# Attention with a top-32 mask and a highway FFN: the pair maxima read PSUM, one evacuation per pair, preparation in pieces late in each period, FFN steps inside the list chain

## The chip, the cores and the metric

The kernel runs on one core of a Trainium2 chip. The metric is device time in microseconds (us) for one launch. The core's engines are TensorE (PE), VectorE (DVE), ScalarE (ACT), GpSimd (POOL) and SyncE (SP), which here only issues DMAs.

## The reference

Attention over 8 batches, 8 heads, 576 rows and a head width of 64, in which each row keeps its 32 largest scores, and then a highway FFN with d_model = 512 on the 4608 rows:

```python
scores = scale * np.matmul(q, k.transpose(0, 1, 3, 2))
kth = np.partition(scores, -top_k, axis=-1)[..., -top_k:-top_k + 1]   # top_k = 32
scores = np.where(scores >= kth, scores, -1000000000.0)
scores = scores - np.max(scores, axis=-1, keepdims=True)
attn = np.exp(scores)
attn = attn / (np.sum(attn, axis=-1, keepdims=True) + 1e-09)
x = np.matmul(attn, v)                  # heads side by side: 4608 x 512
H = np.maximum(x @ w_h, 0.0)
T = 1.0 / (1.0 + np.exp(-(x @ w_t + b_t)))
out = T * H + (1.0 - T) * x
```

## The kernel before

A tile is 128 query rows of one head against all 576 keys. Two tiles make a pair, and there are 144 pairs: 18 for each of the 8 batches. The rows of a batch are cut into groups: four groups of 128 rows with four pairs each, and one remaining group of 64 rows, in whose tiles two heads lie side by side, with two pairs. The main loop runs one step for each pair n, and in this text a step is called a period. Every compute engine takes its instructions in exactly the order in which the loop writes them, so the order of the calls in the loop is the schedule.

What happens to pair n is spread over several periods. `scores` makes q times k for two tiles into two PSUM tiles `ps` (TensorE), and `evac` takes them through a ReLU into the SBUF tile `z` (ScalarE, one instruction for each tile); both are written one period ahead. In period n, `tree` takes the maximum of the two halves of `z` as `hi` and of the two halves of `hi` as `hh` (VectorE), and `minima` makes the matching minima `hl` and `lo` by integer subtraction and addition (GpSimd, four instructions). In period n+1, `lists` runs a chain of MAX8 and MATCH_REPLACE8 for both tiles in turn, which finds the 32nd largest score (`m`, `w`; VectorE). In period n+2, `mask` makes the penalty `pen` = ReLU(threshold - z) (ScalarE), and `trans` transposes z and subtracts a steep multiple of `pen` in PSUM (`zr`, `zt`; TensorE, twenty products), and ScalarE takes the exponential as `et`. In period n+3, `av` multiplies `et` with v and a column of a constant that gives the row's sum (TensorE), and ScalarE copies the result to `xs`.

When a group's last pair has passed `av`, `norm` takes the reciprocal `rinv` (VectorE) and makes `x` (GpSimd), and three FFN jobs are queued, of which each period takes one, behind `lists`: `ffn_x` transposes x (`xtps`), `ffn_h` multiplies with w_h (`hps`) and makes `d` (VectorE), and `ffn_t` multiplies with w_t (`tps`), takes the tanh (ScalarE), updates `d` (VectorE) and adds up `o` (GpSimd, two additions: `o<-x` and `o<-o,d`), which a DMA on SyncE writes. The transposes of x, the three products and those of the preparation share one PSUM tile, `fp`, which has one buffer. `settle` (GpSimd: `room`, `slack`, `reach`) gathers a check for each group; should it fail, an exact version of the whole kernel runs behind the main loop.

The preparation of the next batch, `prep_pair`, loads k, q and v of two heads (`kin`, `qin`, `vin`; twelve DMAs on SyncE), transposes k and q on TensorE (`kqps`) and copies them and v with ScalarE. It is called as a whole, in four of the 18 periods, ahead of that period's `scores`:

```python
            if n in preparing:
                prep(*preparing[n])
            if n == 1:
                load_weights()
            ...
            if have(n + 1):
                g, pi = pairs[n + 1]
                ops.scores(n + 1, g, pi, preps[g.b])
                ops.evac(n + 1)
            if have(n - 1):
                ops.lists(n - 1, *pairs[n - 1])
            for job in ffn[:1]:
                job.pop(0)()
```

The functions that the diff touches, with the lines of the profile (the recording layer at line 35 stands for nearly all instructions there, so rows are told apart by their tiles):

Of the kernel before, what the change touches and what calls it, by code (L numbers as in the profile page):

```python
# [19 lines left out]
J = 4  # L20
# [42 lines left out]
class Ops:  # L63


    def __init__(self, ctx, tc, shared, exact):
# [18 lines left out]
        self.bigps = pool("bigps", 2, space=PS)  # L85
# [7 lines left out]
    def load_pair(self, src, hp, name):  # L93
        nc, D, S, R, P = self.nc, self.D, self.S, self.R, self.P
        JP = J * P
        t = self.ldpool.tile([P, J + 1, 2, D], FP32, tag=name, name=name)
        for hh in range(2):
            h = 2 * hp + hh
            nc.sync.dma_start(
                t[:, 0:J, hh, :], src(h, 0, JP).rearrange("(p j) d -> p j d", j=J)  # L100
            )
            nc.sync.dma_start(t[0:R, J, hh, :], src(h, JP, S))
        return t
# [6 lines left out]
    def prep_pair(self, srcs, hp, prep):  # L110
# [3 lines left out]
        kin = self.load_pair(srcs[1], hp, "kin")  # L114
        qin = self.load_pair(srcs[0], hp, "qin")
        vin = self.load_pair(srcs[2], hp, "vin")
        for src_t, dst_t in ((kin, kT), (qin, qT)):
            kqps = self.fps.tile([P, 512], FP32, tag="fp", name="kqps")
            for c in range(J):
                nc.tensor.transpose(  # L120
                    kqps[:, c * P : (c + 1) * P],
                    src_t[:, c, :, :].rearrange("p h d -> p (h d)"),
                    self.ident[:],
                )
            nc.scalar.copy(dst_t[:, hp, 0:JP], kqps[:])
        kqps = self.fps.tile([P, 512], FP32, tag="fp", name="kqps")
        for i, src_t in enumerate((kin, qin)):
            nc.tensor.transpose(
                kqps[:, i * R : (i + 1) * R],
                src_t[0:R, J, :, :].rearrange("p h d -> p (h d)"),  # L130
                self.ident[0:R, 0:R],
            )
        for i, dst_t in enumerate((kT, qT)):
            nc.scalar.copy(dst_t[:, hp, JP:S], kqps[:, i * R : (i + 1) * R])
        vdst = vb[:, 2 * hp : 2 * hp + 2, :, 0:D].rearrange("p h c d -> p c h d")
        nc.scalar.copy(vdst[:, 0:J], vin[:, 0:J])
        nc.scalar.copy(vdst[0:R, J], vin[0:R, J])
# [3 lines left out]
    def scores(self, n, g, pi, prep):  # L141
# [3 lines left out]
        pss = [  # L145
            self.bigps.tile([P, (J + 1) * P], FP32, tag="big", name="ps")
            for _ in range(2)
        ]
        for s0, s1 in ((0, 512), (512, S)):
            for ti, heads in enumerate(g.pairs[pi]):  # L150
                for hi, h in enumerate(heads):
# [3 lines left out]
                        pss[ti][rows, s0:s1],  # L155
# [3 lines left out]
        self.st[n] = dict(pss=pss)  # L159

    def evac(self, n):
        nc, P, S = self.nc, self.P, self.S
        pss = self.st[n].pop("pss")
        if self.exact:
            sc = self.scpool.tile([P, 2, S], FP32, tag="sc", name="sc")
        else:
            sc = self.zbufs[n % NZ][:, :, 0:S]
        for ti in range(2):
            if self.exact:
                nc.scalar.copy(sc[:, ti, :], pss[ti][:, 0:S])  # L170
            else:
                nc.scalar.activation(sc[:, ti, :], pss[ti][:, 0:S], AF.Relu)
        self.st[n]["sc"] = sc

    def tree(self, n):
# [7 lines left out]
        nc.vector.tensor_tensor(hi[:], sc[:, :, 0:H1], sc[:, :, H1:S], ALU.max)  # L183
# [67 lines left out]
    def lists(self, n, g, pi):  # L251
# [16 lines left out]
        while gens:  # L268
            gens = [x for x in gens if next(x, 0) is None]
# [128 lines left out]
    def ffn_x(self, g):  # L398
# [11 lines left out]
        )  # L410

    def ffn_h(self, g):

        nc, P, n_g, ql = self.nc, self.P, self.n_g, g.qlen
        hps = self.fps.tile([P, 512], FP32, tag="fp", name="hps")
        for i in range(n_g):
            nc.tensor.matmul(
                hps[0:ql, :],
# [15 lines left out]
    def ffn_t(self, g):  # L434

        nc, P, n_g, ql = self.nc, self.P, self.n_g, g.qlen
        tps = self.fps.tile([P, 512], FP32, tag="fp", name="tps")
        for i in range(n_g):
            nc.tensor.matmul(
                tps[0:ql, :],  # L440
# [6 lines left out]
            tps[0:ql, :], self.cst[:, 0:ql], self.bt[:], start=False, stop=True  # L447
        )
        nc.scalar.activation(tps[0:ql, :], tps[0:ql, :], AF.Tanh)
        nc.vector.scalar_tensor_tensor(  # L450
            out=g.d[0:ql, :],
            in0=tps[0:ql, :],
# [6 lines left out]
    def ffn_o(self, g, dst):  # L459
        gp, ql = self.nc.gpsimd, g.qlen  # L460
        o = self.fpool.tile([self.P, self.dm], FP32, tag="o", name="o")
        gp.tensor_tensor(o[0:ql, :], g.x[0:ql, :], g.x[0:ql, :], ALU.add)
        gp.tensor_tensor(o[0:ql, :], o[0:ql, :], g.d[0:ql, :], ALU.add)
# [4 lines left out]
def kernel(  # L468
# [43 lines left out]
    for i in range(2):  # L512
        vt = const([P, H, nck, DE], BF16, f"v{i}")
        nc.gpsimd.memset(vt[:], 2.0)
# [20 lines left out]
    with ExitStack() as cm:  # L535
# [4 lines left out]
        def load_weights():  # L540
            for src, dst in ((moe_w_h, wh), (moe_w_t, wt)):
                for i in range(0, n_g, 2):
# [5 lines left out]
                    weights.append((w32, dst[:, i : i + 2, :], 1.0))  # L548
# [5 lines left out]
            weights.append((bt32, bt[:].unsqueeze(1), 0.5))  # L554
# [24 lines left out]
        preps = {}  # L579

        def prep(b, hp):
            if hp == 0:
                preps[b] = ops.prep_alloc(vbufs[b % 2])
            ops.prep_pair(srcs(b), hp, preps[b])

        preparing = {hp - 1: (0, hp) for hp in range(1, NHP)}
        for b in range(1, B):
            for hp in range(NHP):
                preparing[first[b] - 12 + 3 * hp] = (b, hp)
# [5 lines left out]
        prep(0, 0)  # L595
        ops.scores(0, *pairs[0], preps[0])
        ops.evac(0)
        ffn = []
        step = 0
        while step < NPR + 4 or ffn:  # L600
            n = step
            if have(n):
                ops.tree(n)
                ops.minima(n)
            if have(n - 2):
                ops.mask(n - 2, *pairs[n - 2], tis=(0,))
            if have(n - 3):
# [4 lines left out]
            if n in preparing:  # L612
                prep(*preparing[n])
            if n == 1:
# [112 lines left out]
```

## Time and profile before

| | |
|---|---|
| median of 3 runs | 1103.97 us (1099.82 to 1106.38) |
| the profiled execution | 1100.31 us, of which the trace spans 1098.5 us |
| busy: VectorE, GpSimd, TensorE, ScalarE | 976.7, 839.6, 822.1, 712.1 us |
| mean granted TensorE clock | 0.859 of full speed |
| instructions | 20764 |

Busy time is the union of an engine's instructions. The profile names for each idle time of an engine what ended it, and TensorE's clock is given as a share of full speed.

### The profile page before, as it was taken

To read this page: it belongs to the slowest core of one execution; us is meant where nothing else is said; L and a number is where in the kernel's file an instruction comes from. 1 tells how busy PE (TensorE), PEld (TensorE's weight loads), DVE (VectorE), ACT (ScalarE), POOL (GpSimd) and SP (SyncE) were. 2 spreads that over 40 slices of the span, in tenths; PEclk is the share of its full clock that TensorE was granted. 3 is DMA by queue.
4 is the path that set the end of the run, shared out by engine and by line. 5 is a ranking of instruction groups with operands and counts; after the bars stand their busy time and mean duration, and the time that the engine had idled before them with its cause. 6 is when DMAs were issued, how large, how long until landed. Compare 5 with 4: busy or idle time off the path is not lost.

```text
span 1098.5 us, 20764 instructions
## 1 busy us (share of the span) xinstructions
PE 822.1 (75%) x6562; PEld 549.7 (50%) x6601; DVE 976.7 (89%) x4162; ACT 712.1 (65%) x1425; POOL 839.6 (76%) x842
## 2 busy tenths in 40 slices
PE   5667788778877787777877768786787778777764
PEld 3445455455545555455554545554455445555542
DVE  2699999989998999889998899988999888999992
ACT  3567676667766676567666666676676666766652
POOL 6598788867886778777787777877778776888872
PEclk9988898878887889788897888978799787989886
DMA  4611200122002210121101111011110110000000
GB/s 109 171 34 43 61 25 10 44 59 55 11 17 53 53 44 11 32 57 45 34 10 48 43 43 43 11 38 43 48 39 11 38 43 10 11 11 7 10 20 18
DMA packets 123333, 41.54 MB, mean 38 GB/s; under 512 B 117456, under 2 KB 117456, under 8 KB 123216
## 3 DMA queue, kind: packets, MB, share of 16 engines
q1 hardware_dynamic: 123216, 40.14, 14.6%
q8 instruction: 54, 0.88, 0.3%
q14 instruction: 63, 0.52, 0.2%
HBM read 30.67 MB, written 9.44 MB: 37 GB/s over the span
## 4 chain that ended last, share of the span: by engine, by line
DVE 70%; PE 17%; ACT 8%; issue 3%; SPq 1%; DMA 1%; POOL 0%; ACTq 0%; DVEq 0%; POOLq 0%
DVE w L35 30%; DVE m L35 18%; DVE hh L35 9%; DVE hi L35 8%; PE ps L35 7%; PE kqps L35 5%; DVE d L35 4%; PE tps L35 2%; ACT pen L35 2%; ACT qT L35 2%; ACT kT L35 1%; PE hps L35 1%; ACT tps L35 1%; ACT z L35 1%; PE zt L35 1%
## 5 line engine op out<-in xcount | busy, mean ns | idle before, releaser
L35 ACT ACTIVATE pen<-z,m 128x576 bf16<-128x576 f32 x288 | 223.2, 775 | 142.7 <-DVE m L35 142.7
L35 PE MATMUL ps<-kT,qT 64*128 64x64 f32 (+3 forms) x1280 | 244.6, 509 | 0.0
L35 PE MATMUL zt<-ident,z 128*128 128x128 f32 x1152 | 238.1, 300 | 0.0
L35 DVE MAX8 m<-w 128x8 f32<-128x168 f32 (+1 forms) x864 | 232.6, 309 | 0.0
L35 POOL TENSOR_TENSOR hl<-hi,hh 128x288 int32<-128x288 int32 x144 | 114.2, 793 | 152.7 <-DVE hh L35 152.7
L35 PE MATMUL zt<-nident,pen 128*128 128x128 bf16 x1152 | 226.4, 233 | 0.0
L35 ACT ACTIVATE z<-ps 128x576 f32<-128x576 f32 x288 | 170.9, 646 | 65.1 <-PE ps L35 61.6
L35 POOL TENSOR_TENSOR lo<-lo,z 128x576 int32<-128x576 int32 x144 | 203.6, 1414 | 11.3
L35 POOL TENSOR_TENSOR lo<-z,hi 128x576 int32<-128x576 int32 x144 | 202.8, 1408 | 0.0
L35 ACT ACTIVATE et<-zt 128x512 bf16<-128x512 f32 x288 | 169.3, 605 | 47.9 <-PE zt L35 37.7
L35 PEld LDWEIGHTS zt<-ident,z 128*128 128x128 f32 x1152 | 177.9, 154 | 23.0
L35 PEld LDWEIGHTS ps<-kT,qT 64*128 64x128 f32 (+1 forms) x1280 | 125.9, 206 | 104.5 <-issue 97.5
L35 DVE MATCH_REPLACE8 w<-m,w 128x144 f32<-128x144 f32 (+1 forms) x576 | 170.6, 302 | 0.0
L35 PEld LDWEIGHTS <-pen 128*128 128x128 bf16 x1440 | 162.2, 113 | 9.8 <-ACT pen L35 3.5
L35 DVE TENSOR_TENSOR hi<-z 128x576 f32<-128x576 f32 x144 | 121.7, 845 | 45.7 <-ACT z L35 45.7
L35 PE MATMUL zr<-v,et 128*128 128x65 bf16 (+1 forms) x1600 | 104.0, 200 | 53.5 <-ACT et L35 52.0
L35 DVE TENSOR_TENSOR hh<-hi 128x288 f32<-128x288 f32 x144 | 122.9, 854 | 5.0
L35 POOL TENSOR_TENSOR hl<-hl,hi 128x288 int32<-128x288 int32 x144 | 114.4, 794 | 11.3
L35 PEld LDWEIGHTS <-et 128*128 128x128 bf16 (+1 forms) x1600 | 69.6, 103 | 101.2 <-ACT et L35 98.2
L35 DVE MAX8 w<-lo 128x8 f32<-128x288 f32 x288 | 115.1, 440 | 0.0
L35 POOL TENSOR_TENSOR o<-o,d 128x512 f32<-128x512 f32 (+1 forms) x40 | 65.5, 1637 | 44.9 <-DVE d L35 25.4
L35 DVE MAX8 w<-hl 128x8 f32<-128x72 f32 x576 | 90.3, 217 | 0.0
(62 smaller groups left out, 1169.7 us busy)
## 6 DMA issues: line engine op xcount, KB each, us to landing
kin<-in_k_dram SPq DMA_DIRECT2D x64, 128.0 KB, 2.6
qin<-in_q_dram SPq DMA_DIRECT2D x64, 128.0 KB, 2.6
vin<-in_v_dram SPq DMA_DIRECT2D x64, 128.0 KB, 2.6
out_dram<-o SPq DMA_DIRECT2D x32, 256.0 KB, 2.3
kin<-in_k_dram SPq DMA_DIRECT2D x64, 16.0 KB, 2.3
qin<-in_q_dram SPq DMA_DIRECT2D x64, 16.0 KB, 2.3
vin<-in_v_dram SPq DMA_DIRECT2D x64, 16.0 KB, 2.3
w<-in_moe_w_h_dram SPq DMA_DIRECT2D x2, 512.0 KB, 4.5
```

What stands on the lines that cost most here:

```text
L35: return self._tc.keep_in_program_order(fn(*args, **kw))
```

## The change

It has six parts. (1) `ps` becomes one PSUM tile for both tiles of a pair, in one buffer of four banks where there were two buffers of two; `evac` is one instruction over 2 x 576 elements. (2) `hi` takes its first operand from `ps` and its second from `z`; the ReLU of one side is enough for the maximum. (3) The FFN's products are written ahead of `av`, and the VectorE step that belongs to them after four rounds of the list chain. (4) v's constant column is 1 and not 2, so `x` is whole; ScalarE makes `xh` = x / 2 for `d`, w_h is halved when it is cast, the tanh takes a scale of 0.5, and `o` is one addition of x and d. (5) `prep_pair` gives a list of pieces: the loads are written at least three periods ahead of the first transposes, and the k, the q and the rest go at the end of three periods one after the other. (6) At the start, the first pair's q is loaded from ScalarE's queue, the next head pair's loads are written one step earlier, and the weights' loads come behind the loads of all four head pairs.

```diff
-        self.bigps = pool("bigps", 2, space=PS)
+        self.bigps = pool("bigps", 1, space=PS)
...
+        ps = self.bigps.tile([P, 2, 1024], FP32, tag="big", name="ps")
...
     def evac(self, n):
         nc, P, S = self.nc, self.P, self.S
-        pss = self.st[n].pop("pss")
+        ps = self.st[n]["ps"]
...
-        for ti in range(2):
-            if self.exact:
-                nc.scalar.copy(sc[:, ti, :], pss[ti][:, 0:S])
-            else:
-                nc.scalar.activation(sc[:, ti, :], pss[ti][:, 0:S], AF.Relu)
+            nc.scalar.activation(sc, ps[:, :, 0:S], AF.Relu)
...
-        nc.vector.tensor_tensor(hi[:], sc[:, :, 0:H1], sc[:, :, H1:S], ALU.max)
+        ps = self.st[n].pop("ps")
+        nc.vector.tensor_tensor(hi[:], ps[:, :, 0:H1], sc[:, :, H1:S], ALU.max)
...
+    def run(gens, rounds=99):
+        while gens and rounds:
+            gens[:] = [x for x in gens if next(x, 0) is None]
+            rounds -= 1
...
+        g.xh = self.fpool.tile([P, self.dm], FP32, tag="xh", name="xh")
+        nc.scalar.mul(g.xh[0:ql, :], g.x[0:ql, :], 0.5)
...
-        nc.scalar.activation(tps[0:ql, :], tps[0:ql, :], AF.Tanh)
...
+        nc.scalar.activation(g.ps[0:ql, :], g.ps[0:ql, :], AF.Tanh, scale=0.5)
...
-        gp.tensor_tensor(o[0:ql, :], g.x[0:ql, :], g.x[0:ql, :], ALU.add)
-        gp.tensor_tensor(o[0:ql, :], o[0:ql, :], g.d[0:ql, :], ALU.add)
+        self.nc.gpsimd.tensor_tensor(o[0:ql, :], g.x[0:ql, :], g.d[0:ql, :], ALU.add)
...
-                preparing[first[b] - 12 + 3 * hp] = (b, hp)
+
+                def begin(b=b, hp=hp, f=f):
+                    got = prep(b, hp)
+                    got[0]()
+                    at = f + 3 + 3 * hp
+                    pieces.setdefault(at, []).append(got[1])
+                    pieces.setdefault(at + 1, []).append(got[2])
+                    pieces.setdefault(at + 2, []).append(got[3])
+                    pieces.setdefault(at + 2, []).append(got[4])
+
+                pieces.setdefault(f + 3 * hp, []).append(begin)
...
+            post = None
+            if ffn:
+                pre, post = ffn.pop(0)
+                pre()
             if have(n - 3):
                 g, pi = pairs[n - 3]
                 ops.av(n - 3, g, pi, preps[g.b][2])
             if have(n - 2):
                 ops.mask(n - 2, *pairs[n - 2], tis=(1,))
-            if n in preparing:
-                prep(*preparing[n])
...
-            if have(n - 1):
-                ops.lists(n - 1, *pairs[n - 1])
-            for job in ffn[:1]:
-                job.pop(0)()
-                if not job:
-                    ffn.pop(0)
+            gens = ops.lists(n - 1, *pairs[n - 1]) if have(n - 1) else []
+            ops.run(gens, 4)
+            if post:
+                post()
+            ops.run(gens)
             if have(n - 2):
                 ops.trans(n - 2)
+            for piece in pieces.pop(n, []):
+                piece()
```

Here f is the number of the batch's first pair less 17, `got[0]` the loads, `got[1]` and `got[2]` the transposes and copy of k and q, `got[3]` those of the last 64 rows and `got[4]` the copies of v. The pairs (`pre`, `post`) are (`ffn_x`, nothing), (`ffn_h`, `ffn_d`) and (`ffn_t`, `ffn_e` and `ffn_o`).

On VectorE, in a period with the FFN's first product, before: from the last lists of a pair (`w<-hl`, `w<-lo`) over the FFN step `d` to the next pair's maximum `hi`.

```order
L35 MAX w_3348<-hl 128x8 x4
L35 MAX w_3348<-lo 128x8 x2
L35 MAX m_3683<-w_3348 128x8
L35 MAX m_3685<-w_3348 128x8
L35 MATCH_REPLACE w_3687<-m_3683,w_3348 128x168
L35 MATCH_REPLACE w_3689<-m_3685,w_3348 128x168
L35 MAX m_3347<-w_3687 128x8
L35 MAX m_3347<-w_3689 128x8
L35 SCALAR_TENSOR_TENSOR d<-hps,x 128x512
L35 TENSOR_TENSOR hi<-z_75 128x576
L35 TENSOR_TENSOR hh<-hi 128x288
```

And in the same place of the changed kernel, from a pair's `hi` on:

```order
L35 TENSOR_TENSOR hi<-ps,z_73 128x576
L35 TENSOR_TENSOR hh<-hi 128x288
L35 MAX m_3309<-hh 128x8 x2
L35 MATCH_REPLACE w_3611<-m_3309,hh 128x144
L35 MATCH_REPLACE w_3613<-m_3309,hh 128x144
L35 MAX m_3310<-w_3611 128x8
L35 MAX m_3310<-w_3613 128x8
L35 MATCH_REPLACE w_3312<-m_3310,w_3611 128x144
L35 MATCH_REPLACE w_3312<-m_3310,w_3613 128x144
L35 SCALAR_TENSOR_TENSOR d<-hps,xh 128x512
L35 MAX w_3312<-hl 128x8 x4
```

`d` has moved from the end of the chain, ahead of the next `hi`, to a place behind the second MATCH_REPLACE of both tiles; and `hi` reads `ps` beside `z`.

On TensorE, in a period with preparation, before: the end of the attention values (`zr<-v,et`), the transposes of k and q, and the scores `ps`.

```order
L35 LDWEIGHTS et
L35 MATMUL zr<-v_85,et 128x65
L35 MATMUL kqps<-ident,kin 128x128 x4
L35 MATMUL kqps<-ident,qin 128x128 x4
L35 MATMUL kqps<-ident,kin 128x64
L35 MATMUL kqps<-ident,qin 128x64
L35 MATMUL ps<-kT,qT 128x512 x2
L35 MATMUL ps<-kT,qT 128x64 x2
```

After, at the end of one of the three periods with a piece of the same head pair, the one with the last 64 rows: the end of the transposes, the piece, then the next period's FFN job (here the transposes of x) and its attention values, behind which come the scores.

```order
L35 LDWEIGHTS pen_79
L35 MATMUL zt<-nident,pen_79 128x128
L35 MATMUL kqps<-ident,kin 128x64
L35 MATMUL kqps<-ident,qin 128x64
L35 MATMUL xtps<-ident,x 128x128 x4
L35 LDWEIGHTS et
L35 MATMUL zr<-v_85,et 128x65
```

The preparation has left the place ahead of the scores for one behind the transposes, and an FFN job stands in front of the attention values and the scores.

On ScalarE, in a period with the tanh (`tps<-tps`), before: penalties, copy of the attention values, evacuation `z`, tanh, exponentials.

```order
L35 ACTIVATE pen_79<-z_67,m_5833 128x576
L35 COPY xs<-zr 128x130
L35 ACTIVATE pen_79<-z_67,m_5833 128x576
L35 ACTIVATE z_73<-ps 128x576 x2
L35 ACTIVATE tps<-tps 128x512
L35 ACTIVATE et<-zr 128x2x128
L35 ACTIVATE et<-zt 128x512 x2
```

After, in such a period, from the preparation's copy on:

```order
L35 COPY qT<-kqps 128x512
L35 ACTIVATE pen_79<-z_73,m_11672 128x576
L35 ACTIVATE tps<-tps 64x512
L35 COPY xs<-zr 128x130
L35 ACTIVATE pen_79<-z_73,m_11672 128x576
L35 ACTIVATE z_67<-ps 128x2x576
L35 ACTIVATE et<-zr 128x2x128
L35 ACTIVATE et<-zt 128x512 x2
```

The tanh stands ahead of the evacuation and not behind it, the copy of the preparation ahead of the penalties, and the evacuation is one instruction.

## Rows read from the trace of the kernel before

**Rows 1.** The page's first part: busy time of each engine.

```profile
PE 822.1 (75%) x6562; PEld 549.7 (50%) x6601; DVE 976.7 (89%) x4162; ACT 712.1 (65%) x1425; POOL 839.6 (76%) x842
```

**Rows 2.** VectorE's waits: us in total, times, longest us.

```profile
DVE hi L35 <- ACT z L35: 45.7, 12, 11.3
DVE d L35 <- ACT tps L35: 42.5, 17, 3.5
DVE d L35 <- PE hps L35: 19.0, 8, 5.0
```

**Rows 3.** VectorE's timeline: start, us, instruction, idle time before it.

```profile
42.79 0.76 DVE L35 TENSOR_TENSOR hi<-z 128x576 f32<-128x576 f32 x1 [7.98 <-ACT z L35]
...
400.32 0.76 DVE L35 TENSOR_TENSOR hi<-z 128x576 f32<-128x576 f32 x1 [2.56 <-ACT z L35]
...
533.31 0.76 DVE L35 TENSOR_TENSOR hi<-z 128x576 f32<-128x576 f32 x1 [2.58 <-ACT z L35]
...
1080.06 0.69 DVE L35 SCALAR_TENSOR_TENSOR d<-hps,x 128x512 f32<-128x512 f32 x1 [5.00 <-PE hps L35]
...
1089.77 0.68 DVE L35 SCALAR_TENSOR_TENSOR d<-tps,d 64x512 f32<-64x512 f32 x1 [3.03 <-ACT tps L35]
```

**Rows 4.** VectorE's timeline, two periods of the steady part.

```profile
539.83 0.75 DVE L35 TENSOR_TENSOR hi<-z 128x576 f32<-128x576 f32 x1
540.62 0.46 DVE L35 TENSOR_TENSOR hh<-hi 128x288 f32<-128x288 f32 x1
...
545.76 0.67 DVE L35 SCALAR_TENSOR_TENSOR d<-tps,d 128x512 f32<-128x512 f32 x1
546.35 0.95 DVE L35 TENSOR_TENSOR hi<-z 128x576 f32<-128x576 f32 x1
547.33 1.41 DVE L35 TENSOR_TENSOR hh<-hi 128x288 f32<-128x288 f32 x1
```

**Rows 5.** Instructions of tile `hi`: ns minimum, median and maximum.

```profile
L35 DVE TENSOR_TENSOR hi<-z x144: 697/748/1617, 13.0 to 1061.1; 128x576 f32<-128x576 f32 x144
L35 DVE TENSOR_TENSOR hh<-hi x144: 457/459/1550, 13.8 to 1061.9; 128x288 f32<-128x288 f32 x144
```

**Rows 6.** Groups by form: busy us, mean ns of one, idle time before.

```profile
L35 DVE TENSOR_TENSOR hh<-hi 128x288 f32<-128x288 f32 x144 | 122.9, 854 | 5.0
L35 DVE TENSOR_TENSOR hi<-z 128x576 f32<-128x576 f32 x144 | 121.7, 845 | 45.7 <-ACT z L35 45.7
```

**Rows 7.** GpSimd's timeline beside the second period of rows 4.

```profile
545.63 1.05 POOL L35 TENSOR_TENSOR o<-x 128x512 f32<-128x512 f32 x1
546.87 1.56 POOL L35 TENSOR_TENSOR o<-o,d 128x512 f32<-128x512 f32 x1 [0.19 <-POOL o L35]
```

**Rows 8.** TensorE's timeline at the start.

```profile
35.37 1.09 PE L35 MATMUL kqps<-ident,kin 128*128 128x128 f32 x4 [7.83 <-DMA kin<-in_k_dram]
```

**Rows 9.** TensorE's timeline in the steady part.

```profile
522.49 0.63 PE L35 MATMUL kqps<-ident,kin 128*128 128x128 f32 x4
...
528.15 4.05 PE L35 MATMUL ps<-kT,qT 64*64 64x512 f32 x16
...
535.45 2.17 PE L35 MATMUL ps<-kT,qT 64*64 64x512 f32 x16
...
541.24 1.30 PE L35 MATMUL ps<-kT,qT 64*128 64x512 f32 x8
...
543.56 0.27 PE L35 MATMUL zr<-ident,z 128*128 128x128 f32 x1
...
545.43 0.33 PE L35 MATMUL zr<-v,et 128*128 128x65 bf16 x5
```

**Rows 10.** Stretches: length; busy PE, PEld, DVE, ACT, POOL; granted clock; DMA.

```profile
528.20:532.10 3.90, 3.90 (x17) 1.38 (x16) 2.53 (x12) 1.05 (x5) 2.28 (x2) 0.51 0.35 78
...
953.20:956.50 3.30, 1.25 (x7) 1.19 (x8) 3.27 (x19) 2.26 (x6) 3.22 (x6) 0.81 0.02 5
956.50:959.80 3.30, 3.15 (x30) 2.43 (x28) 3.30 (x11) 2.01 (x5) 3.09 (x3) 0.67 0.00 0
```

More of the change, by code (lines that the diff above doesn't have):

```diff
@@ L113, in prep_pair, with load, main @@
         kT, qT, vb = prep
[L114 to L117, printed above, removed]
+        ins = {}
+        def load():
+            ins["k"] = self.load_pair(srcs[1], hp, "kin")
+            ins["q"] = self.load_pair(srcs[0], hp, "qin", qeng)
+            ins["v"] = self.load_pair(srcs[2], hp, "vin")
+        def main(name, dst):
             kqps = self.fps.tile([P, 512], FP32, tag="fp", name="kqps")
@@ L121, in prep_pair, with last, values @@
                     kqps[:, c * P : (c + 1) * P],
-                    src_t[:, c, :, :].rearrange("p h d -> p (h d)"),
+                    ins[name][:, c, :, :].rearrange("p h d -> p (h d)"),
                     self.ident[:],
                 )
[L125 to L137, printed above, removed]
+            nc.scalar.copy(dst[:, hp, 0:JP], kqps[:])
+        def last():
+            kqps = self.fps.tile([P, 512], FP32, tag="fp", name="kqps")
+            for i, name in enumerate("kq"):
+                nc.tensor.transpose(
+                    kqps[:, i * R : (i + 1) * R],
+                    ins[name][0:R, J, :, :].rearrange("p h d -> p (h d)"),
+                    self.ident[0:R, 0:R],
+                )
+            for i, dst in enumerate((kT, qT)):
+                nc.scalar.copy(dst[:, hp, JP:S], kqps[:, i * R : (i + 1) * R])
+        def values():
+            vdst = vb[:, 2 * hp : 2 * hp + 2, :, 0:D].rearrange("p h c d -> p c h d")
+            nc.scalar.copy(vdst[:, 0:J], ins["v"][:, 0:J])
+            nc.scalar.copy(vdst[0:R, J], ins["v"][0:R, J])
+        return [load, lambda: main("k", kT), lambda: main("q", qT), last, values]
     def scores(self, n, g, pi, prep):
@@ L267, in lists @@
             ]
-        while gens:
-            gens = [x for x in gens if next(x, 0) is None]
+        return gens
+    @staticmethod
+    def run(gens, rounds=99):
+        while gens and rounds:
+            gens[:] = [x for x in gens if next(x, 0) is None]
+            rounds -= 1
     def settle(self, g):
@@ L579, with prep @@
         preps = {}
-        def prep(b, hp):
+        pieces = {}
+        def prep(b, hp, qeng=None):
             if hp == 0:
                 preps[b] = ops.prep_alloc(vbufs[b % 2])
-            ops.prep_pair(srcs(b), hp, preps[b])
-        preparing = {hp - 1: (0, hp) for hp in range(1, NHP)}
+            return ops.prep_pair(srcs(b), hp, preps[b], qeng)
         for b in range(1, B):
+            f = first[b] - 17
             for hp in range(NHP):
-                preparing[first[b] - 12 + 3 * hp] = (b, hp)
+                def begin(b=b, hp=hp, f=f):
[7 more added lines that the diff above has]
+                pieces.setdefault(f + 3 * hp, []).append(begin)
         NPR = len(pairs)
@@ L593, in have @@
             return 0 <= n < NPR
-        prep(0, 0)
+        early = [prep(0, hp, nc.scalar if hp == 0 else None) for hp in range(NHP)]
+        early[0][0]()
+        early[1][0]()
+        for piece in early[0][1:4]:
+            piece()
         ops.scores(0, *pairs[0], preps[0])
         ops.evac(0)
+        early[0][4]()
         ffn = []
@@ L601 @@
             n = step
+            if n + 1 < NHP:
+                for piece in early[n + 1][1:4]:
+                    piece()
+                if n + 2 < NHP:
+                    early[n + 2][0]()
+            if n == 1:
+                load_weights()
             if have(n):
@@ L604 @@
                 ops.minima(n)
+            if weights and n > 2:
+                cast_weights()
             if have(n - 2):
                 ops.mask(n - 2, *pairs[n - 2], tis=(0,))
+            post = None
+            if ffn:
+                pre, post = ffn.pop(0)
+                pre()
             if have(n - 3):
@@ L675 @@
                 for hp in range(NHP):
-                    ops.prep_pair(srcs, hp, pr)
+                    for piece in ops.prep_pair(srcs, hp, pr):
+                        piece()
                 outb = out.rearrange("(b s) n -> b s n", b=B)
@@ L683 @@
                         ops.evac(n)
-                        ops.lists(n, g, pi)
+                        ops.run(ops.lists(n, g, pi))
                         ops.mask(n, g, pi)
```

78 lines of the change are left out of this document (41 added, 37 removed).

## The prediction

> **What bounds the kernel now.** I read the page's busy shares first, then VectorE's waits, then its instructions in order of time. VectorE is busy for 976.7 of 1098.5 us [rows 1], more than any other engine, so the kernel lasts as long as VectorE's work and its waits. Those waits have only three names [rows 2]: the pair maximum `hi` waits for ScalarE's evacuation `z` (45.7 us, 12 times), and the two FFN steps `d` wait for the tanh (42.5 us) and for the first product (19.0 us). The timeline shows where they are [rows 3]: the batch from 400.32 to 533.31 us lasts 133.0 us and ends with a `hi` wait of 2.58. It belongs to the period whose loading and transposing (prep) stands ahead of the scores on TensorE. Elsewhere VectorE works without a gap. An undisturbed period runs from the `hi` at 539.83 to the `d` at 545.76, so a pair costs 5.93 us, and a `d` adds 0.59 (545.76 to 546.35) [rows 4].
>
> Part of the busy time is waiting too. `hh` has a median of 0.459 us but a mean of 0.854; `hi` has 0.748 and 0.845 [rows 5, 6]. The long ones lie beside GpSimd's work: the `hi` at 546.35 takes 0.95 us while GpSimd's `o<-x` ends, and the `hh` at 547.33 takes 1.41 us, to 0.31 us behind the end of `o<-o,d` at 548.43 [rows 4, 7]. But the `d` at 545.76, which reads one operand from PSUM, takes 0.67 us for 512 elements, though `o<-x` runs beside it [rows 4, 7]; that is no more per element than an undisturbed `hi`. So in these rows an operation with two SBUF operands is held up by GpSimd, and one with a PSUM operand is not. Over 144 pairs the excess is 144 x (0.854 - 0.459) = 56.9 us for `hh` and 144 x (0.845 - 0.748) = 14.0 us for `hi`.
>
> **The change, part by part,** against the profiled execution's 1100.31 us (span 1098.5 and 1.8 around it).
>
> *Start: -7.8.* The fourth pair's `hi` starts only at 42.79 us [rows 3], because TensorE waits 7.83 us for `kin` [rows 8], whose loads stand on SyncE behind those of the weights. Now the weights come behind all four head pairs: 42.79 - 7.83 = 34.96. Bounds: 5, if another load is then late, and 10, as the first q's four issues leave SyncE for ScalarE's queue as well.
>
> *`hi` waits: -17.9.* In seven batches prep no longer stands ahead of the scores. 45.7 less the four of the start (27.8 together, the last of them 7.98 [rows 3]; the part above deals with them) leaves 17.9.
>
> *`d` waits: -49.0.* The products now run ahead of the attention-value products, and `d` stands behind four rounds of the list chain, about 3 us into the period. 42.5 + 19.0 = 61.5; four of these waits, from 5.00 to 3.03 us and 12.5 together, lie in the tail behind the last pair [rows 3], where nothing covers them, and stay.
>
> *Maxima from PSUM: -14.0.* By the `d` row, `hi` will no longer be held up. Has a PSUM read a price of its own? `hh` (288 elements, 0.459) and `hi` (576, 0.748) [rows 5] put 512 elements at 0.684 us on a straight line, and the `d` takes 0.67 [rows 4]. So I charge nothing; the bounds of the gain are 0 (still held up) and 14. [...]
>
> *`hh`: -30.* One of the two `o` additions goes, and the other is issued mid-chain. GpSimd's minima of a pair start with the end of `hh` and end 4.5 us later, where `o` starts (from 540.62 + 0.46 to 545.63) [rows 4, 7]. An `o` of 1.05 to 1.56 [rows 7] then ends before or just as the next `hh` starts, 6.2 us behind the last one's end. What stays is `x`: it starts as the chain ends and, with its 512 elements, takes about the 1.05 of `o<-x`; `hh` comes 0.8 us later and waits about 0.45: 40 x 0.45 = 18. Five weight casts at about 1 and eight `x` that follow `settle` at about 0.5 make 9 more. 56.9 - 27 = 30. Bounds: 0 and 45.
>
> *Evacuation, halved x, prep pieces: 0.* One evacuation of 1152 elements follows the scores where two did. ScalarE is busy for 712 us [rows 1], and its 40 halvings lie beside VectorE's chain; without that cover they would cost 40 times some 1.05 us at most, by `o<-x` again. Prep is the same work, moved behind the transposes.
>
> *New waits: +20.* This is the price of the change. Scores n+1 now need the one PSUM tile, which VectorE's `hi` n releases, so TensorE can't run ahead; and the FFN product that waits for `x` stands in front of the scores. Queued behind that wait are the attention values, the scores, the evacuation, and so the next `hi`. At the full clock eight score products take 1.30 us, the twenty transposes 1.87 (543.56 to 545.43), the attention values two times 0.33, an FFN job about 1.0 (between scores and transposes) and a prep piece 0.63 [rows 9]: 5.5 us against VectorE's 5.93 to 6.5. Counted from `hi` in an `x` period: `x` lands at 1.25 us, its four transposes end at 2.0, the attention values at 2.7, the scores at 4.0, the evacuation (twice 0.65 in one) at 5.25. The next `hi` is due at 5.93 + 0.45 and more, so it holds by about 1 us. At the low clock it doesn't: sixteen score products took 4.05 us at 0.51 of full speed, and 2.17 a period later [rows 9, 10], so the sum comes out about 2 us late. When does the clock fall? It was 0.81 and 0.67 in two stretches from 953.2 us, in the first of which TensorE was busy for only 1.25 of 3.3 us [rows 10]. Such a dip cost VectorE nothing there (busy for 3.27 and 3.30). In the new order the one long empty stretch in a batch is ahead of an `x` in a period with neither FFN nor prep. I take one dip a batch at 2 us, and 0.5 us for a `d` that comes too early: 8 x 2.5 = 20. [...]
>
> *Tail: -1,* the addition that goes.
>
> Sum: 1100.3 - 7.8 - 17.9 - 49.0 - 14.0 - 30 - 1 = 980.6 without new waits, 1000.6 with them. The profiled execution lay 3.7 us under the median of the runs, which scatter over 6.6 us; I put the median at 1003.
>
> **The rivals.**
> *No new waits.* The spread-out prep keeps TensorE busy enough for the full clock throughout: 981. For it: TensorE's work moves evenly into the periods. Against: the empty stretch of each batch stays.
> [...]
> *GpSimd still holds up both maxima.* 14 + 30 come back: 1045. For it: `hh` keeps two SBUF operands, and a faster VectorE reaches it before GpSimd is through. Against: the `d` row.
> [...]
>
> **How the numbers follow.** Likeliest, 0.52, is that VectorE stays the bound with few new waits: 1003, by itself 988 to 1030. No new waits 0.12, score tile 0.20, GpSimd 0.10, slower 0.06. Between 975 and 1055 lie nearly all of the first two, most of the GpSimd case and the lower part of the score-tile case, about 8 in 10. A measurement of this kernel tells about 0.5%, 5.5 us, from no change. All cases but the slower one end further below than that, and a part of that one lies near no change: faster 0.94, same 0.02, slower 0.04.
>
> **What would show it.** Right: all `hi` at about 0.75 us; `hh`'s mean near 0.65; `d` waiting only in the tail; the fourth `hi` near 35 us; batches of about 118 us; a mean granted clock above 0.9. Wrong: `hi` waiting for `z` in many periods, and TensorE's scores for `hi`, which is the score tile; `d` waiting for the tanh mid-chain; `hh` as long as before beside `x` and `o`.

## The result and the profile after

The changed kernel takes 984.07 us (median; 981.76 to 984.19) against 1104.28 us (1099.82 to 1106.38) in the same comparison: a ratio of 0.891, 95% interval 0.888 to 0.894. The profiled execution took 983.99 us with a span of 982.1, against 1100.31 before. The mean granted clock rose from 0.859 to 0.902.

The page's busy time of each engine, after (against [rows 1]):

```profile
PE 757.5 (77%) x6601; PEld 528.8 (54%) x6601; DVE 926.1 (94%) x4162; ACT 711.4 (72%) x1321; POOL 762.0 (78%) x802
```

VectorE is still the bound and now busy for 94% of the span, with 50.6 us less of busy time for the same 4162 instructions (57.5 without its first one, `nident`, which is recorded 6.90 us longer; see the experiments). Its waits after, in us in total, times, longest (against [rows 2]):

```profile
DVE hi L35 <- ACT z L35: 26.7, 16, 6.6
DVE d L35 <- PE hps L35: 10.1, 5, 6.7
DVE d L35 <- ACT tps L35: 4.3, 2, 3.0
```

The waits for the tanh have all but gone (42.5 to 4.3). Those of `hi` have not: 12 waits became 16. The instructions of tile `hi` after, in ns (against [rows 5]), and below them the same two as groups with busy us and mean ns (against [rows 6]):

```profile
L35 DVE TENSOR_TENSOR hi<-ps,z x144: 697/734/758, 12.9 to 943.7; 128x576 f32<-128x576 f32 x144
L35 DVE TENSOR_TENSOR hh<-hi x144: 457/459/1142, 13.7 to 944.4; 128x288 f32<-128x288 f32 x144
```

```profile
L35 DVE TENSOR_TENSOR hi<-ps,z 128x576 f32<-128x576 f32 x144 | 105.2, 730 | 26.7 <-ACT z L35 26.7
L35 DVE TENSOR_TENSOR hh<-hi 128x288 f32<-128x288 f32 x144 | 82.8, 575 | 5.0
```

No `hi` takes over 758 ns any more, where the longest took 1617; and the 575 of `hh` is less than I had forecast. VectorE's timeline after (start, us, instruction, idle time before it; against [rows 3]) gives the stages:

```profile
1.43 7.23 DVE L520 TENSOR_SCALAR nident<-ident 128x128 bf16<-128x128 f32 x1 [1.43 <-POOL ident masks.py:199]
12.94 0.76 DVE L35 TENSOR_TENSOR hi<-ps,z 128x576 f32<-128x576 f32 x1 [4.28 <-ACT z L35]
...
34.55 0.76 DVE L35 TENSOR_TENSOR hi<-ps,z 128x576 f32<-128x576 f32 x1 [1.97 <-ACT z L35]
...
72.16 0.76 DVE L35 TENSOR_TENSOR hi<-ps,z 128x576 f32<-128x576 f32 x1 [6.61 <-ACT z L35]
...
149.28 0.76 DVE L35 TENSOR_TENSOR hi<-ps,z 128x576 f32<-128x576 f32 x1 [0.35 <-ACT z L35]
...
265.43 0.76 DVE L35 TENSOR_TENSOR hi<-ps,z 128x576 f32<-128x576 f32 x1 [0.35 <-ACT z L35]
...
465.33 0.78 DVE L35 TENSOR_TENSOR hh<-hi 128x288 f32<-128x288 f32 x1
...
472.77 0.76 DVE L35 TENSOR_TENSOR hi<-ps,z 128x576 f32<-128x576 f32 x1 [1.90 <-ACT z L35]
...
820.95 0.76 DVE L35 TENSOR_TENSOR hi<-ps,z 128x576 f32<-128x576 f32 x1 [1.89 <-ACT z L35]
...
964.30 0.69 DVE L35 SCALAR_TENSOR_TENSOR d<-hps,xh 128x512 f32<-128x512 f32 x1 [6.65 <-PE hps L35]
```

The first two rows are needed further down. The fourth `hi` starts at 34.55 us (42.79 before). The 18 pairs of a batch, from the third `hi` of one batch to the third of the next, take 265.43 - 149.28 = 116.2 us (133.0 for 18 pairs before). The last row stands in the tail. The waits at 72.16, 472.77 and 820.95 are new, and TensorE's timeline shows where they come from (the two rows from 234.47 on are the same place of another batch):

```profile
66.95 1.11 PE L35 MATMUL xtps<-ident,x 128*128 128x128 f32 x4 [10.09 <-POOL x L35]
...
234.47 0.65 PE L35 MATMUL xtps<-ident,x 128*128 128x128 f32 x4 [2.88 <-POOL x L35]
...
235.37 2.17 PE L35 MATMUL ps<-kT,qT 64*64 64x512 f32 x16
...
462.36 0.60 PE L35 MATMUL kqps<-ident,qin 128*128 128x128 f32 x4
465.85 1.11 PE L35 MATMUL xtps<-ident,x 128*128 128x128 f32 x4 [2.89 <-POOL x L35]
...
467.45 4.10 PE L35 MATMUL ps<-kT,qT 64*64 64x512 f32 x16
```

The transposes of x now stand ahead of the scores and wait for GpSimd's `x`: 2.89 us at 465.85, 10.09 at 66.95. Behind the wait at 465.85 the scores run slowly: 16 products take 4.10 us; in the kernel before they took 2.17 [rows 9], at a granted clock of 1.00. The windows of that period (length; busy PE, PEld, DVE, ACT, POOL; granted clock; DMA) show the clock:

```profile
464.00:467.50 3.50, 1.65 (x16) 1.50 (x16) 3.47 (x16) 1.27 (x3) 2.69 (x4) 0.67 0.01 3
467.50:471.60 4.10, 4.10 (x18) 1.49 (x18) 3.37 (x19) 1.45 (x4) 3.12 (x3) 0.50 0.02 4
```

TensorE had ended a piece of prep at 462.96 and stood empty until 465.85. The mean granted clock is 0.67 in the first window and 0.50 in the second. The same empty stretch doesn't always end so: behind the 2.88 us at 234.47 the scores take 2.17 us, at a granted clock of 1.00, and `hi` doesn't wait. At this place of the eight batches the scores ran at 0.50 twice, ahead of the `hi` at 472.77 and of that at 820.95; why in these two is not shown. And GpSimd's timeline:

```profile
63.12 2.77 POOL L35 TENSOR_SCALAR wt<-w 128x1024 bf16<-128x1024 f32 x1
...
65.85 1.05 POOL L35 TENSOR_TENSOR x<-xs,rinv 128x512 f32<-128x512 f32 x1
...
464.75 1.04 POOL L35 TENSOR_TENSOR x<-xs,rinv 128x512 f32<-128x512 f32 x1 [0.33 <-DVE rinv L35]
```

The first `x` is late because a weight cast of 2.77 us stands ahead of it on GpSimd.

### The profile page after: what moved, and what is told of

Its sections match the earlier page's. It is cut to its first block, busy times and chain, and to the rows that moved or that the text cites. A ratio compares the mean times of both kernels' runs of the same rounds, so it can differ in the third digit from the quotient of the medians.

```text
span 982.1 us, 20525 instructions
## 1 busy us (share of the span) xinstructions
PE 757.5 (77%) x6601; PEld 528.8 (54%) x6601; DVE 926.1 (94%) x4162; ACT 711.4 (72%) x1321; POOL 762.0 (78%) x802
## 4 chain that ended last, share of the span: by engine, by line
DVE 80%; PE 8%; POOL 6%; ACT 2%; SPq 2%; issue 1%; DMA 1%; POOLq 0%; DVEq 0%
DVE w L35 37%; DVE m L35 22%; DVE hi L35 8%; DVE hh L35 7%; DVE d L35 5%; PE ps L35 4%; POOL lo L35 2%; PE zr L35 2%; PE xtps L35 1%; POOL x L35 1%; ACT z L35 1%; POOL hl L35 1%; SPq L103 1%; PE zt L35 1%; SPq L100 1%
## 5 line engine op out<-in xcount | busy, mean ns | idle before, releaser
L35 PE MATMUL ps<-kT,qT 64*128 64x64 f32 (+3 forms) x1280 | 236.2, 497 | 61.8 <-DVE hi L35 61.6
L35 PE MATMUL zt<-ident,z 128*128 128x128 f32 x1152 | 232.2, 295 | 0.0
L35 PE MATMUL zt<-nident,pen 128*128 128x128 bf16 x1152 | 220.7, 229 | 0.0
L35 ACT ACTIVATE z<-ps 128x1152 f32<-128x1152 f32 x144 | 162.9, 1131 | 74.1 <-PE ps L35 72.5
L35 PEld LDWEIGHTS ps<-kT,qT 64*128 64x128 f32 (+1 forms) x1280 | 117.6, 200 | 170.5 <-issue 97.5
L35 DVE TENSOR_TENSOR hi<-ps,z 128x576 f32<-128x576 f32 x144 | 105.2, 730 | 26.7 <-ACT z L35 26.7
L35 PE MATMUL xtps<-ident,x 128*128 128x128 f32 (+1 forms) x160 | 31.7, 333 | 94.8 <-POOL x L35 91.3
L35 PEld LDWEIGHTS <-et 128*128 128x128 bf16 (+1 forms) x1600 | 74.2, 108 | 38.5 <-ACT et L35 15.4
L35 PE MATMUL zr<-v,et 128*128 128x65 bf16 (+1 forms) x1600 | 86.9, 203 | 6.0 <-ACT et L35 4.0
L35 DVE TENSOR_TENSOR hh<-hi 128x288 f32<-128x288 f32 x144 | 82.8, 575 | 5.0
```

The costliest lines, as they stand in the source:

```text
L35: return self._tc.keep_in_program_order(fn(*args, **kw))
```

## The experiments

Each kernel is either the changed one ("after") or the one before, with one edit. Sums go against the profiled executions (983.99 and 1100.31 us); "ratio" is to the kernel before, with its 95% interval. One thing helps in reading them. The very first `hi` starts at 13 us everywhere (12.94 after), but waits 4.28 us after and 11.26 before, since the instruction ahead of it on VectorE (`nident`) is recorded as 7.23 us after and 0.33 before; so I leave its wait out of the sums. (It is 0.33 in e6 and 7.23 in e4 and e10 too, so the order of the kernel doesn't decide it.) Without it `hi` waits 34.4 us before and 22.4 after.

**e1: after, `hi` from SBUF alone.** What is the operand in PSUM worth?

```diff
-        ps = self.st[n].pop("ps")
-        nc.vector.tensor_tensor(hi[:], ps[:, :, 0:H1], sc[:, :, H1:S], ALU.max)
+        self.st[n].pop("ps")
+        nc.vector.tensor_tensor(hi[:], sc[:, :, 0:H1], sc[:, :, H1:S], ALU.max)
```

> The changed kernel, but the first maximum takes both halves from z in SBUF again; ps is then free once ScalarE has evacuated it. Theory (the PSUM operand frees VectorE from GpSimd): hi goes from a mean of 0.730 back to about 0.75 to 0.85 us and hh from 0.575 to about 0.66, since x can't start until hi is through: 144 x 0.03 to 0.1 and 40 x 0.3, so 15 to 25 us slower than the changed kernel, about 1003 us, ratio to the kernel before 0.904 to 0.914. Rival (the one tile handed over by VectorE is the dearer side, and the operand's place is nothing): the 62 us that the scores wait for hi go, hi's waits for z go with them, and the time stays or falls, 975 to 985, ratio 0.883 to 0.892.

1035.55 us, ratio 0.939 (0.937 to 0.942). Instructions of tiles `hi` and `x` in e1 (ns):

```profile
L35 DVE TENSOR_TENSOR hi<-z x144: 700/744/2062, 13.0 to 995.2; 128x576 f32<-128x576 f32 x144
```

```profile
L35 POOL TENSOR_TENSOR x<-xs,rinv x40: 1035/1447/1456, 66.9 to 1017.1; 128x512 f32<-128x512 f32 x32, 64x512 f32<-64x512 f32 x8
```

and its waits on VectorE, with one of TensorE's rows ahead of such a wait:

```profile
DVE hi L35 <- ACT z L35: 48.1, 28, 5.6
```

```profile
490.45 1.11 PE L35 MATMUL xtps<-ident,x 128*128 128x128 f32 x4 [4.51 <-POOL x L35]
```

The long `hi` are back, up to 2062 ns; their busy time is 132.1 us against 105.2, so 26.9 of the loss. In 30 of them it is `o` beside which they are long, in 7 it is `x`. `x`, which runs beside `hi`, has a median of 1447 ns here against 1042 after: each holds up the other. TensorE now waits for `x` for 154.0 us in all, where it was 91.3: at the place of the row shown 4.51 us, where it was 2.89. Behind that row 16 score products take 4.10 us, as at the granted clock of 0.50 after, and the next `hi` waits 1.89 us. A wait of 1.89 or 1.90 us comes once in each of the eight batches, where it came in two. These six more batches are about 11 of the 21.4 us that `hi` waits more. With 2.7 us of `hh` that is 51.0 of the 51.5 us measured. The direction was the theory's, the size was over twice as large.

**e4: before, one score tile, one evacuation, `hi` half from PSUM;** prep and FFN stay where they were.

```diff
-        pss = [
...
+        ps = self.bigps.tile([P, 2, 1024], FP32, tag="big", name="ps")
...
+            nc.scalar.activation(sc, ps[:, :, 0:S], AF.Relu)
...
-        nc.vector.tensor_tensor(hi[:], sc[:, :, 0:H1], sc[:, :, H1:S], ALU.max)
+        ps = self.st[n].pop("ps")
+        nc.vector.tensor_tensor(hi[:], ps[:, :, 0:H1], sc[:, :, H1:S], ALU.max)
```

> The kernel before with only the score tile of a pair in one buffer, one evacuation and the first maximum half from PSUM; prep, FFN and o as before. Theory (the operand's place saves the contention, the hand-over costs little): hi saves 16 us and hh up to 16 where x starts earlier, and the one tile costs up to 15 us in the periods with prep ahead of the scores: 1075 to 1095, ratio 0.975 to 0.99. Rival (the one tile costs more than it gives without the other parts, as prep ahead of the scores can't be run ahead of): 1105 to 1150, ratio 1.0 to 1.04.

1047.34 us, ratio 0.949 (0.946 to 0.952). VectorE's waits, and the two groups with busy us and mean ns:

```profile
DVE hi L35 <- ACT z L35: 41.2, 12, 7.6
DVE d L35 <- ACT tps L35: 26.0, 15, 3.7
DVE d L35 <- PE hps L35: 13.1, 10, 4.9
```

```profile
L35 DVE TENSOR_TENSOR hi<-ps,z 128x576 f32<-128x576 f32 x144 | 105.6, 733 | 41.2 <-ACT z L35 41.2
L35 DVE TENSOR_TENSOR hh<-hi 128x288 f32<-128x288 f32 x144 | 105.4, 732 | 5.0
```

`hi` loses 16.1 us of busy time, `hh` 17.5, the `d` waits 22.4, and `hi` waits 2.4 longer: 53.6 in all; the profiled execution lies 53.1 below that of before, again more than the theory's range. A third of it is in the instruction that was changed.

**e11: e4 with `hi` from SBUF,** so one tile and one evacuation alone. Against e4:

```diff
-        ps = self.st[n].pop("ps")
-        nc.vector.tensor_tensor(hi[:], ps[:, :, 0:H1], sc[:, :, H1:S], ALU.max)
+        self.st[n].pop("ps")
+        nc.vector.tensor_tensor(hi[:], sc[:, :, 0:H1], sc[:, :, H1:S], ALU.max)
```

> The kernel before with one PSUM tile for both score tiles and one evacuation, but the first maximum from z in SBUF as before. Theory (the 55 us that the kernel before gained from the maximum half from PSUM come from the operand's place): nothing is gained, and a few us may be lost as scores can't be a tile ahead, 1100 to 1115, ratio 0.998 to 1.013. Rival (the single evacuation or the later scores made part of the 55 us): 1060 to 1090, ratio 0.96 to 0.99.

1099.33 us, ratio 0.997 (0.995 to 1.000). So the gain of e4 is the operand's, and the one score tile costs nothing here. But here ScalarE's evacuation releases the tile, and TensorE never waits for it; in e4, where `hi` releases it, TensorE's scores wait for `hi` for 76.1 us in all, and what that costs is part of e4's gain and not measured by itself.

**e2: after, the whole FFN job behind scores and chain,** where it was before.

```diff
-            post = None
-            if ffn:
-                pre, post = ffn.pop(0)
-                pre()
...
-            ops.run(gens, 4)
-            if post:
-                post()
             ops.run(gens)
+            if ffn:
+                pre, post = ffn.pop(0)
+                pre()
+                if post:
+                    post()
```

> The changed kernel, but each FFN job whole at its old place: products behind the scores, the VectorE step behind the whole list chain. Theory (the steps mid-chain removed the d waits): waits of d for the tanh and the first product come back with at most the 49 us of before, and o meets hh again (16 to 30 us); as prep no longer piles up ahead of the scores, I expect 10 to 25 us of the waits: together 25 to 55 us slower than the changed kernel, 1010 to 1040, ratio 0.915 to 0.94. Rival (the d waits came from prep ahead of the scores, and went with it): no d waits come back outside the tail, at most the o contention is paid: below 1000, ratio under 0.906.

982.82 us, ratio 0.892 (0.889 to 0.894): no change to after. VectorE's waits, and the group `hh`:

```profile
DVE hi L35 <- ACT z L35: 12.5, 4, 5.6
DVE d L35 <- PE hps L35: 7.2, 3, 3.7
DVE d L35 <- ACT tps L35: 4.8, 2, 3.0
```

```profile
L35 DVE TENSOR_TENSOR hh<-hi 128x288 f32<-128x288 f32 x144 | 97.2, 675 | 5.0
```

The `d` waits don't come back: my theory fell. Two effects cancel: `hi` waits 14.2 us less, since x no longer stands ahead of the scores, and `hh` is 14.4 us longer, since `o` is issued later and meets it (36 `hh` are long beside an `o`, in the changed kernel none).

**e9: before, prep in late pieces** (with loads ahead of time for the later batches); FFN, tiles and the start's order of work stay.

```diff
-                preparing[first[b] - 12 + 3 * hp] = (b, hp)
...
+                pieces.setdefault(f + 3 * hp, []).append(begin)
...
+            for piece in pieces.pop(n, []):
+                piece()
```

> The kernel before with only the preparation of later batches in pieces behind the transposes and loaded early; score tiles, FFN and o as before. Theory (prep ahead of the scores made the waits of d as well as those of hi, since a d waits for products that TensorE reaches only behind prep and the scores): of 61.5 us of d waits only the 12.5 of the tail stay, the 17.9 of hi go, GpSimd's share of hi and hh stays: 1030 to 1045, ratio 0.935 to 0.95. Rival (the d waits belong to the place of the FFN steps): only the hi waits go, 1078 to 1085, ratio 0.98 to 0.985.

1045.67 us, ratio 0.949 (0.947 to 0.952). VectorE's waits:

```profile
DVE hi L35 <- ACT z L35: 27.6, 4, 14.3
DVE d L35 <- ACT tps L35: 10.7, 9, 3.0
DVE d L35 <- PE hps L35: 7.7, 2, 5.0
```

`hi` waits only at the start. And the `d` waits are down from 61.5 to 18.4, with every FFN step at its old place. At the start the edit costs something: the next batch's first loads now stand on SyncE ahead of those of the fourth head pair, TensorE waits up to 13.0 us for `kin` (7.83 before [rows 8]), and the fourth `hi` starts at 49.27 us (42.79 before), so behind the start the gain is about 61 us and not 55.

**e10: before, FFN products ahead of the attention values, `d` mid-chain;** prep stays whole and ahead of the scores, and `o` keeps its two additions.

```diff
+            post = None
+            if ffn:
+                pre, post = ffn.pop(0)
+                pre()
             if have(n - 3):
...
-            if have(n - 1):
-                ops.lists(n - 1, *pairs[n - 1])
-            for job in ffn[:1]:
-                job.pop(0)()
...
+            gens = ops.lists(n - 1, *pairs[n - 1]) if have(n - 1) else []
+            ops.run(gens, 4)
+            if post:
+                post()
+            ops.run(gens)
```

> The kernel before with only the FFN products ahead of the attention values and the steps d mid-chain; score tiles, preparation and the two additions for o as before. Theory (prep is what is late): TensorE still stands in prep ahead of the scores, and now also waits for x there, so the waits change their name from d to hi and the time falls little or rises: 1080 to 1120, ratio 0.98 to 1.015. Rival (the place of the FFN steps made the d waits): the 49 us go, 1045 to 1060, ratio 0.95 to 0.963.

1168.12 us, ratio 1.060 (1.057 to 1.063), slower than my range. VectorE's waits, TensorE's wait for `d`, and its timeline in a period with prep:

```profile
DVE hi L35 <- ACT z L35: 176.5, 43, 7.7
DVE d L35 <- PE hps L35: 8.4, 2, 6.2
DVE d L35 <- ACT tps L35: 7.1, 6, 3.0
```

```profile
PE kqps L35 <- DVE d L35: 83.3, 20, 4.9
```

```profile
515.30 0.87 PE L35 MATMUL kqps<-ident,kin 128*128 128x128 f32 x4 [4.95 <-DVE d L35]
...
518.91 2.34 PE L35 MATMUL ps<-kT,qT 64*128 64x512 f32 x7
```

The `d` waits go (61.5 to 15.5 with 8.4 for the first product), and `hi` waits 137.6 us more. The product holds the tile `fp`, which has one buffer, until `d` has read it mid-chain; prep needs the same tile and waits 4.95 us for `d`; the scores stand behind prep. Such a collision precedes 20 of the `hi` waits, which come to 92.0 us. The seven longest behind the start (5.5 to 5.9 us) come without one: there prep stands behind a wait for `x`, and the scores behind both. In e9, with prep late in the period, TensorE waits for `d` there as well (64.7 us, 21 times), and yet `hi` waits only at the start. `hi` and `hh` are 25.2 us shorter: 137.6 - 46.0 - 25.2 = 66.4 of the 67.7 us measured.

**e3: after, prep whole and ahead of the scores again** (loads still early).

```diff
-                    pieces.setdefault(at, []).append(got[1])
...
+                    whole[f + 5 + 3 * hp] = got[1:]
...
+            for piece in whole.pop(n, []):
+                piece()
             if have(n + 1):
```

> The changed kernel, but the transposes and copies of a head pair whole and ahead of the scores in one period, as before; the loads stay early. Theory (pieces late in the period took prep off the path): about 5 us of transposes and copies in turns stand ahead of the scores in four periods of a batch; with one score tile and a slack of 1 to 2 us each costs 2 to 4 us, 28 times: 55 to 110 us slower than the changed kernel, 1040 to 1095, ratio 0.94 to 0.99. Rival (the loads were what was late, or TensorE's slack covers it): at most the 18 us of hi waits of before come back, ratio up to 0.908.

1108.52 us, ratio 1.006 (1.004 to 1.008): without the pieces nothing of the change's gain is left. VectorE's and TensorE's longest waits:

```profile
DVE hi L35 <- ACT z L35: 148.9, 41, 6.1
```

```profile
PE kqps L35 <- DVE d L35: 75.1, 20, 4.6
```

This is more than my range. The same collision as in e10 precedes 20 of the `hi` waits (87.0 us); the 122.2 us of new `hi` waits are nearly the whole 125.8 lost. Prep whole is not enough for that: e4 has it too, with the FFN at its old place, and takes 1047.34 us.

**e8: after, an extra addition of 512 elements ahead of `o` on GpSimd;** its result is overwritten.

```diff
+        gp.tensor_tensor(o[0:ql, :], g.x[0:ql, :], g.x[0:ql, :], ALU.add)
         gp.tensor_tensor(o[0:ql, :], g.x[0:ql, :], g.d[0:ql, :], ALU.add)
```

> The changed kernel with a second GpSimd addition of 512 elements ahead of the one that makes o (its result is overwritten, the output is the same). Theory (hh was relieved because one addition fits between the minima and the next hh, and two don't): o ends about 1 us later and meets hh 40 times, 0.5 to 1 us each: 20 to 40 us slower than the changed kernel, 1003 to 1023, ratio 0.907 to 0.926. Rival (it is the place mid-chain that counts, and GpSimd has room for both): under 5 us, ratio 0.889 to 0.896.

1029.75 us, ratio 0.936 (0.932 to 0.940). GpSimd's timeline, and VectorE's beside it:

```profile
506.00 1.05 POOL L35 TENSOR_TENSOR o<-x 128x512 f32<-128x512 f32 x1
507.12 1.27 POOL L35 TENSOR_TENSOR o<-x,d 128x512 f32<-128x512 f32 x1
```

```profile
507.49 1.21 DVE L35 TENSOR_TENSOR hh<-hi 128x288 f32<-128x288 f32 x1
```

`hh` ends 0.31 us behind `o` (508.70 and 508.39), as before [rows 4, 7]. Its mean is 737 ns: 23.4 us more. The other 19.9 us are `hi` waits, 46.6 in place of 26.7: TensorE waits for `x` for 131.7 us in all where it was 91.3, and `hi` waits 1.89 or 1.90 us once in six batches, where it did in two. Forty additions of 1.04 us cost 45.6, somewhat more than the theory's 20 to 40.

**e5, e6, e7: the new waits.** e5 casts the weights on ScalarE (first edit); e6 puts the transposes of x behind the scores (second edit); e7 does both.

```diff
-            ops.nc.gpsimd.tensor_scalar_mul(dst, w32[:], by)
+            ops.nc.scalar.mul(dst, w32[:], by)
...
-                        (lambda g=g: ops.ffn_x(g), None),
+                        (lambda: None, lambda g=g: ops.ffn_x(g)),
```

> The changed kernel, but ScalarE casts the weights and the bias, not GpSimd. Theory (the 6.6 us wait of hi at 72 us comes from x queued on GpSimd behind the casts, with the FFN job that needs x ahead of the scores on TensorE): that wait goes, and so does what hh waits for beside the casts: 6 to 9 us faster than the changed kernel, 975 to 978, ratio 0.883 to 0.886. Rival (it is a late load or the shared FFN tile): nothing changes, ratio 0.889 to 0.893.

> The changed kernel, but the transposes of x stand behind the scores on TensorE, so that nothing that waits for x stands ahead of them; the other two FFN jobs stay early. Theory (the waits of hi that are left come from x ahead of the scores): the 6.6 us at the start and most of the other 7.5 us of hi waits go: 8 to 14 us faster than the changed kernel, 970 to 976, ratio 0.879 to 0.884. Rival (they come from low clock stretches alone, which stay): only the 6.6 us go or nothing, ratio 0.884 to 0.892.

> The changed kernel with both: ScalarE casts the weights, and the transposes of x stand behind the scores. Theory: both ways lead to the same 6.6 us, so the two together are hardly better than the better one alone, 970 to 975, ratio 0.878 to 0.883. Rival (they add up): ratio 0.872 to 0.877.

e5: 975.41 us, ratio 0.886 (0.883 to 0.890). e6: 969.93, 0.881 (0.877 to 0.885). e7: 962.62, 0.8745 (0.8707 to 0.8782), the best version of all: it beats both kernels. VectorE's waits in e6, and TensorE's longest:

```profile
DVE hi L35 <- ACT z L35: 19.4, 4, 11.3
```

```profile
PE ps L35 <- DVE hi L35: 127.0, 92, 2.6
```

In e6 `hi` waits only at the start: the 14.1 us of its waits behind it (26.7 less the four of the start, 12.6) are gone, and the time falls by 14.3. Now TensorE waits for `hi`, 127.0 us in all, which costs VectorE nothing: outside the start no `hi` waits for its scores. But the late `x` at 66 us still finds a victim in e6:

```profile
73.62 0.69 DVE L35 SCALAR_TENSOR_TENSOR d<-hps,xh 128x512 f32<-128x512 f32 x1 [4.57 <-PE hps L35]
```

Only moving the cast takes that away, which is why e7 gains more than e6 alone, where I had taken the two for the same 6.6 us. In e7 VectorE is busy for 924.0 us, 96% of the span.

## Why the prediction was right, and where it was not

The forecast of 1003 us (975 to 1055) lay 19 us above the median. By the terms, from the 1100.31 us of the profiled execution:

| term | forecast | measured | from |
|---|---|---|---|
| start | -7.8 | -8.2 | fourth `hi`: 42.79 to 34.55 |
| old `hi` waits behind the start | -17.9 | -17.9 | 45.7 - 27.8, all counted as gone; e9 |
| `d` waits outside the tail | -49.0 | -49.0 | all counted as gone; new ones below |
| new waits | +20 | +15.6 | `hi` 14.1, `d` 1.2, `lo` 0.3 |
| `hi` | -14.0 | -16.5 | 121.7 to 105.2 |
| `hh` | -30 | -40.1 | 122.9 to 82.8 |
| tail | -1 | +1.0 | last `hi` to the end: 37.4 to 38.4 |
| sum | -99.7 | -115.1 | times: -116.3 |

**`hh` was mis-sized most.** I left 27 us of excess, 22 beside `x` and 5 beside the casts; 16.7 stay: 144 x (0.575 - 0.459). Of these 15.9 are the 37 `hh` beside an `x`, none is beside an `o`, as forecast, and 0.9 are left for all else. Beside most `x`, `hh` takes 0.78 us (465.33), 0.32 more and not the 0.45 that I took; it ends 0.32 us behind the end of `x` (466.11 and 465.79), sooner than its undisturbed 0.46.

**The `d` waits had the right size and the wrong cause.** The step "the products now run ahead of the attention-value products, and `d` stands behind four rounds of the list chain" was to bring the 49 us. It is not needed for them: with the step undone they stay away (e2). Alone it does take the `d` waits away (e10: from 61.5 to 15.5), but only to bring more of `hi`, and the kernel is 6% slower. They go without it with prep in late pieces (e9: to 18.4) and in part with the operand in PSUM (e4: to 39.1): as I read it, with prep and a slow `x` out of the way, the FFN's products come early enough at the old place too; no run shows that step by itself. What the early FFN does bring is 14 us of shorter `hh`, since `o` ends sooner (675 against 575 ns in e2), and it costs 14 us of `hi` waits, as x stands ahead of the scores. e6 keeps the one without the other.

**The operand in PSUM was worth more than its term.** By e1 it carries 51 us of the new order, by e4 against e11 some 52 of the old one, of which the 14 that I charged to `hi` are a part. I had the direct hold-up and left out its other side, the GpSimd operation that becomes shorter (1447 to 1042 ns), and the scores that wait for it. The longest `hi` is 758 ns with one SBUF operand (after) and 2062 with two (e1). I had charged no price for the read from PSUM, and none shows: the median is 734 ns with the operand in PSUM and 748 [rows 5] with both in SBUF.

**The new waits came to about the sum forecast, and that is luck.** The mechanism forecast is there: an empty TensorE ahead of `x`, a low clock (0.50), scores of 4.10 us, and then 1.90 us of `hi` wait, the 2 us that I took. But I counted on it in each of eight batches, and it came in two (472.77 and 820.95). Instead of the other six came a wait that I had not seen, 6.61 us at 72.16, behind a weight cast ahead of the first `x` (gone in e5). The rest are waits of 0.88 us and less, as at 149.28 and 265.43. With x behind the scores all of them vanish (e6), so x ahead of the scores is needed for them; e6 doesn't tell the wait for x from the low clock behind it. And I had put the empty stretch into a period with neither FFN nor prep, where it comes right behind a piece of prep (462.36).

**The rivals.** The time of "No new waits" (981) is that of e6, by another way (x moved, the mean granted clock still at 0.92); it ends lower still, at 970, because `hh` gained 9.5 us and `hi` 2.7 more than forecast. The score-tile case (0.20), in which the single tile `ps` binds, and the slower one (0.06) rest on my assumption that a low clock costs time in a large part of the periods, which no run of the changed kernel shows: behind the scores at a granted clock of 0.50 `hi` waits 1.90 us at 472.77 and 1.89 at 820.95, and all its waits behind the start come to 14.1 us, at a mean clock of 0.902. Both cases are out: in e6 TensorE waits 127.0 us for `hi` to release the tile, at 970 us. "GpSimd still holds up both maxima" is out by the `hi` rows. What I missed among them is a collision on `fp`: in e3 and e10, with the FFN early and prep ahead of the scores, 87.0 and 92.0 us of `hi` waits stand behind it.

**Left open.** The new start was not run by itself. Why the clock fell to 0.50 in two of the eight batches, and not in four others with the same empty stretch of 2.9 us, is not known. Two score tiles with the rest of the change were not tried either. The single gains don't add up: e4 and e9 alone bring 53 and 55 us, and e8 and e1 put 46 and 51 on parts that overlap with them; only the table above is a sum.

## What to carry to other kernels

Where a bound engine's instructions have a mean far above their median, look whether the long ones end just behind those of a neighbour. Here one operand in PSUM ended that for `hi` (at most 758 ns, 1617 before), the hold-up had run both ways (`x` at 1447 and 1042 ns), and what was gained outside the instruction itself, with what the neighbour then delivered sooner, came to 37.5 of 53.6 us in e4 and 24.6 of 51.5 in e1. Before an operation is moved earlier, list what shares its PSUM buffer and what stands behind that on its queue: the same move cost 6% alone (e10) and nothing beside the other parts of the change (e2). Work that waits for another engine belongs behind the work that the bound engine waits for, as in e6.

## What the runs showed of the hardware that I had not expected

GpSimd's `x` took 1447 ns (median) beside a `hi` with both operands in SBUF and 1042 beside one with an operand in PSUM, so the contention shows on both engines. The hold-up ends at a steady distance: before, the 37 `hh` that are long beside `o<-o,d` end 0.31 to 0.32 us behind it, and in e1 the 30 `hi`, of twice the size, that are long beside `o` end 0.61 to 0.62 us behind it. And VectorE's first instruction, a 128x128 TENSOR_SCALAR, is recorded as 7.23 us in the changed kernel and in most of the variants, 0.33 in the kernel before and in e6, 6.92 in e9 and 6.61 in e11, with the first `hi` at 13 us in all; why is open.
